# Two matmuls of 256 columns in place of one of 512 in a float32r kernel of an attention and two MLPs

## The chip, the cores and the metric

The kernel runs on one core of one Trainium2 chip. The metric is the device time of one execution in microseconds. A TensorE (PE) matmul multiplies a weight tile that lies in the array with the columns of a second tile; in the profile the loading of the weights has a row of its own, PEld. The other engines are VectorE (DVE), ScalarE (ACT), GpSimd (POOL) and SyncE (SP, which starts the DMAs here).

## What is computed

There are 12480 tokens with 128 channels. An attention with 32 inducing points goes over them twice, and two MLPs with 2048 hidden units follow:

```python
h = mab(I, x)                                   # 32 inducing points attend to all tokens
x = mab(x, h)                                   # the tokens attend to the 32 results
h = x @ w_in                                    # first MLP, 128 -> 2048
g = np.maximum(h, 0.0) + alpha * np.minimum(h, 0.0)
x = g @ w_out                                   # 2048 -> 128
h = np.maximum(x @ w2_in, 0.0)                  # second MLP, 128 -> 2048
return h * h @ w2_out                           # 2048 -> 128
```

`mab` is a softmax attention without projections.

## The kernel before

The tokens are cut into 25 tiles: 24 of T = 512 tokens and a last one of 192. A first stage, up to about 45 us, transposes the tokens (L244), computes the first attention and folds its result into the weights of the first MLP, so that this MLP can start from the attention weights `a_s` of a tile.

The main loop then runs in steps; step s handles one chunk of 128 hidden units of one tile, 16 chunks a tile and 400 steps' worth of chunks (25 x 16). All big products of the loop are in the type float32r, a fast form of float32 of lower precision. To keep the accuracy, an operand is split into two parts (`hi` and `lo`), and the function `three` (L588 to L591) forms a product from three matmuls into the same PSUM bank: weight hi x data hi, weight lo x data hi, weight hi x data lo. In each step, in this order:

- `l1_a` (matmul in L579) forms the chunk of the first hidden layer, one matmul, whose weights and data hold hi and lo parts in different partitions. ACT takes its relu into `g1h` (L583), DVE the remainder into `g1l` (L585).
- `l2_a`, 24 chunks behind, forms a chunk of the second hidden layer with `three`; ACT takes the relu `r` (L623), DVE multiplies to `sq` (L625).
- `l2_split` rounds `sq` to `g2h` on ACT (L632) and the remainder to `g2l` on POOL (L634).
- `l1_b`, 3 to 5 chunks behind `l1_a`, adds the chunk to the tile's first output (bank `y1`) with `three`.
- `l2_b`, 4 chunks behind `l2_a`, adds the chunk to the tile's second output (bank `y2`) with `three`; after the last chunk the tile is stored.

That is one matmul plus three times three, so ten matmuls of 512 columns in a step. Once a tile `end_y1` adds one more (L607), for the linear part of the first activation. A table (`plan`) puts the leftover work of the weights (conversion from the raw words, splitting, loads) and the attention of later tiles (L440 and following) between the steps, after their matmuls. The order of each engine is the order in which the code issues; nothing is rearranged. Every product writes a PSUM bank of its own of 512 float32 columns: two banks each for `h1`, `h2` and `y2`, one for `y1`. The profile leaves the numbers out of names, so `h` stands for both `h1` and `h2`, `y` for `y1` and `y2`.

Of the kernel before, what the change touches and what calls it, by code (L numbers as in the profile page):

```python
# [26 lines left out]
def attention_then_two_mlps(ctx: ExitStack, tc, x, inducing, w_in, w_out, alpha, w2_in, w2_out, out):  # L27
# [3 lines left out]
    nc = tc.nc  # L31
# [3 lines left out]
    P = 128  # L35
# [27 lines left out]
    def free_bank():  # L63
        turn[0] += 1
        return ms_bank() if turn[0] % 2 or main_loop else y2_bank()
# [3 lines left out]
    def keep_tile(name, shape, dt=F32):  # L69
        return keep.tile(shape, dt, name=name, tag=name)  # L70
# [35 lines left out]
    w1s = keep_tile("w1s", [P, DFF], F32R)  # L106
# [9 lines left out]
    v_s = keep_tile("v_s", [P, P], F32R)  # L116
# [132 lines left out]
    def scores(lhsT, tiles):  # L249
        b = free_bank()  # L250
        for i, t in enumerate(tiles):
            nc.tensor.matmul(  # L252
                b[i * M : (i + 1) * M, : geo[t][1]], lhsT, xt_cols(t), start=True, stop=True,
                tile_position=(0, i * M),
            )
        return b
# [82 lines left out]
    b = free_bank()  # L339
    nc.tensor.transpose(b[:, :M], ind, ident[:M, :M])  # L340
    nc.vector.tensor_copy(indT, b[:, :M])
    for g in range(last):
        b = scores(indT, groups[g])
# [31 lines left out]
    b = free_bank()  # L375
# [5 lines left out]
    b = scores(indT, groups[last])  # L381
# [4 lines left out]
    b = free_bank()  # L386
# [9 lines left out]
    b = free_bank()  # L396
# [11 lines left out]
    b = free_bank()  # L408
# [8 lines left out]
    b = y1_bank()  # L417
# [153 lines left out]
    y1_cur, y2_cur, y1_split = {}, {}, {}  # L571
    g1, g2, rr = {}, {}, {}

    def l1_a(i, other_bank):
        t, c = divmod(i, NCH)
        w = geo[t][1]
        b = h2_bank() if other_bank else h1_bank()
        a = a_s[t]
        nc.tensor.matmul(b[:, :w], w1s[: a.shape[0], c * P : (c + 1) * P], a[:, :w], start=True, stop=True)  # L579

        tag = "g2" if i < EARLY and i % 2 else "g1"
        hi = wk.tile([P, T], F32R, name="g1h", tag=tag + "h", bufs=4)[:, :w]
        nc.scalar.activation(hi, b[:, :w], AF.Relu)  # L583
        lo = wk.tile([P, T], F32R, name="g1l", tag=tag + "l", bufs=4)[:, :w]
        nc.vector.scalar_tensor_tensor(lo, b[:, :w], 0.0, f32(hi), op0=ALU.max, op1=ALU.subtract)  # L585
        g1[i] = hi, lo

    def three(b, w_hi, w_lo, hi, lo, start, stop):  # L588
        nc.tensor.matmul(b, w_hi, hi, start=start, stop=False)  # L589
        nc.tensor.matmul(b, w_lo, hi, start=False, stop=False)  # L590
        nc.tensor.matmul(b, w_hi, lo, start=False, stop=stop)  # L591

    def l1_b(i):
        t, c = divmod(i, NCH)
        if c == 0:
            y1_cur[t] = y1_bank() if t != 1 else y2_bank()
        b = y1_cur[t][:, : geo[t][1]]
        hi, lo = g1.pop(i)
        three(b, wo_hi[:, c, :], wo_lo[:, c, :], hi, lo, c == 0, False)
        if c == NCH - 1 and t:  # L600
            end_y1(t)

    def end_y1(t):
        w = geo[t][1]
        b = y1_cur.pop(t)[:, :w]
        a = a_s.pop(t)
        nc.tensor.matmul(b, v_s[: a.shape[0]], a[:, :w], start=False, stop=True)  # L607
        hi = wk.tile([P, T], F32R, name="y1h", tag="y1h", bufs=2)[:, :w]
        nc.scalar.copy(hi, b)
        lo = wk.tile([P, T], F32R, name="y1l", tag="y1l", bufs=2)[:, :w]  # L610
        nc.vector.tensor_tensor(lo, b, f32(hi), op=ALU.subtract)  # L611
        y1_split[t] = hi, lo

    def l2_a(i):
        t, c = divmod(i, NCH)
        w = geo[t][1]
        b = h2_bank()[:, :w]
        cols = slice(c * P, (c + 1) * P)
        three(b, w2[0][:, cols], w2[1][:, cols], *y1_split[t], True, True)
        if c == NCH - 1:  # L620
            del y1_split[t]
        r = wk.tile([P, T], F32, name="r", tag="r", bufs=2)[:, :w]
        nc.scalar.activation(r, b, AF.Relu)  # L623
        sq = wk.tile([P, T], F32, name="sq", tag="sq", bufs=3)[:, :w]
        nc.vector.tensor_tensor(sq, b, r, op=ALU.mult)  # L625
        rr[i] = sq
# [10 lines left out]
    def l2_b(i):  # L637
        t, c = divmod(i, NCH)
        t0, w, _, rs = geo[t]
        if c == 0:  # L640
            y2_cur[t] = y2_bank()
        b = y2_cur[t][:, :w]
        hi, lo = g2.pop(i)
        cols = slice(c * P, (c + 1) * P)
        three(b, w2[2][:, cols], w2[3][:, cols], hi, lo, c == 0, c == NCH - 1)
        if c == NCH - 1:


            o = wk.tile([P, T], F32, name="o", tag="o", bufs=2)[:, :w]
            nc.vector.transpose(o, b)  # L650
            del y2_cur[t]
            dst = out[t0 : t0 + w, :].rearrange("(b i r) (a j) -> a i r b j", i=M, j=M, r=rs)
            for a in range(P // M):
                nc.sync.dma_start(
                    out=dst[a], in_=o[a * M : (a + 1) * M, :].rearrange("i (r b j) -> i r b j", r=rs, j=M)
                )
# [36 lines left out]
    at(19, copy_u)  # L693
    at(20, step_v)
    at(22, end_y1, 0)
    for tiles in groups[1:]:
        for k, v in enumerate(second_attention(tiles)):
# [34 lines left out]
    for s in range(total + LAG2 + LAG2B + 4):  # L732
        if s < total:
            l1_a(s, s < LAG2 and s % 2)
        if 0 <= s - LAG2 < total:
            l2_a(s - LAG2)
        if 0 <= s - LAG2 - 1 < total:
            l2_split(s - LAG2 - 1)

        ends = [(l1_b, i) for i in l1_b_at.get(s, [])]  # L740
        if 0 <= s - LAG2 - LAG2B < total:
            ends.insert(0 if ends and ends[0][1] % NCH == 0 else len(ends), (l2_b, s - LAG2 - LAG2B))
        for f, i in ends:
            f(i)
        for f in plan.pop(s, []):
            f()
# [30 lines left out]
```

## Time and profile before

| what | us |
|---|---|
| median of 3 runs | 1006.49 (1006.4 to 1009.52) |
| the profiled execution, its time | 1006.87 |
| its span, first to last instruction | 1005.1 |
| PE busy in the span | 983.9 (98%) |
| DVE / ACT / POOL busy | 665.7 / 736.3 / 545.6 |

Matmuls are pipelined: the record of one ends after the next one's record has begun, so the listed durations add up to more than the time in which they ran. The distance from one start to the next is what a matmul takes from the engine. A weight load is listed apart and runs beside matmuls.

### The profile page before, as it was taken

Reading aid. Unit: us, or ns where it says so; the run is one execution under the profiler, and the core shown is the slowest. Engines: PE = TensorE matmul, PEld = TensorE weight load, DVE = VectorE, ACT = ScalarE, POOL = GpSimd, SP = SyncE. Lnnn points to the kernel's source line nnn. Section 1 sums busy time; section 2 is a strip of 40 time slices with the busy share of each in tenths; the row PEclk is TensorE's granted clock in tenths of the full one; section 3 lists DMA queues with packets and bytes.
Section 4 is the critical chain, followed back from the end, with each engine's and each line's share of the span. In section 5 each row is a group of like instructions: output and inputs, shape, how many; then the busy total and the mean of one; then the engine's idle time right before and its main releaser. Section 6 shows DMA issues by size and latency. Waiting matters only on the chain.

```text
span 1005.1 us, 13640 instructions
## 1 busy us (share of the span) xinstructions
PE 983.9 (98%) x4526; PEld 777.5 (77%) x4526; DVE 665.7 (66%) x1042; ACT 736.3 (73%) x1354; POOL 545.6 (54%) x436
## 2 busy tenths in 40 slices
PE   7879999999999999999999999999999999999997
PEld 5456788888788888788888788888788888788886
DVE  5799776666676666666666666666666666666556
ACT  5688877777777777777777777777777777777775
POOL 1346965555556555556555556555556555555560
PEclk9899999999999999999999999999999999999999
DMA  8513001100001100000100000100000200000000
GB/s 295 172 50 108 1 11 30 24 11 6 6 11 27 27 11 1 11 11 20 33 11 1 11 11 14 40 11 1 11 11 9 45 12 1 11 11 4 11 12 15
DMA packets 65062, 28.20 MB, mean 28 GB/s; under 512 B 53584, under 2 KB 57952, under 8 KB 64992
## 3 DMA queue, kind: packets, MB, share of 16 engines
q1 hardware_dynamic: 64992, 27.33, 10.9%
q8 instruction: 35, 0.57, 0.2%
q14 instruction: 35, 0.29, 0.1%
HBM read 14.80 MB, written 6.39 MB: 21 GB/s over the span
## 4 chain that ended last, share of the span: by engine, by line
PE 94%; DVE 3%; issue 1%; ACT 1%; DMA 0%; POOL 0%; SPq 0%; DVEq 0%; POOLq 0%; ACTq 0%
PE y L590 18%; PE y L591 18%; PE y L589 18%; PE h L589 9%; PE h L591 9%; PE h L590 9%; PE h L579 9%; PE h L244 1%; DVE g1l L585 1%; DVE mag L182 1%; PE ms L440 1%; PE y L607 1%; PE ms L252 0%; PE y L317 0%; DMA xg<-in_x_dram 0%
## 5 line engine op out<-in xcount | busy, mean ns | idle before, releaser
L634 POOL TENSOR_TENSOR g2l<-sq,g2h 128x512 fp32r<-128x512 f32 x376 | 487.7, 1297 | 370.1 <-ACT g2h L632 370.1
L585 DVE SCALAR_TENSOR_TENSOR g1l<-h,g1h 128x512 fp32r<-128x512 f32 (+1 forms) x400 | 269.5, 676 | 243.1 <-ACT g1h L583 239.9
L583 ACT ACTIVATE g1h<-h 128x512 fp32r<-128x512 f32 (+1 forms) x400 | 235.3, 589 | 164.4 <-PE h L579 162.7
L625 DVE TENSOR_TENSOR sq<-h,r 128x512 f32<-128x512 f32 (+1 forms) x400 | 270.8, 677 | 65.4 <-ACT r L623 8.9
L623 ACT ACTIVATE r<-h 128x512 f32<-128x512 f32 (+1 forms) x400 | 235.6, 589 | 72.3 <-PE h L591 71.6
L632 ACT CAST g2h<-sq 128x512 fp32r<-128x512 f32 (+1 forms) x400 | 240.5, 601 | 1.6 <-DVE sq L625 1.6
L579 PE MATMUL h<-a_s,w1s 128*128 128x512 f32 (+2 forms) x400 | 158.0, 396 | 6.3 <-DVE g1l L585 3.7
L589 PE MATMUL h<-y1h,w2i_hi 128*128 128x512 f32 (+1 forms) x400 | 157.7, 394 | 0.6 <-DVE g1l L585 0.3
L591 PE MATMUL h<-y1l,w2i_hi 128*128 128x512 f32 (+1 forms) x400 | 156.8, 392 | 0.4 <-DVE y1l L611 0.4
L589 PE MATMUL y<-g2h,w2o_hi 128*128 128x512 f32 (+1 forms) x400 | 157.0, 393 | 0.0
L591 PE MATMUL y<-g2l,w2o_hi 128*128 128x512 f32 (+1 forms) x400 | 156.9, 392 | 0.0
L590 PE MATMUL y<-g2h,w2o_lo 128*128 128x512 f32 (+1 forms) x400 | 156.8, 392 | 0.0
L590 PE MATMUL h<-y1h,w2i_lo 128*128 128x512 f32 (+1 forms) x400 | 156.7, 392 | 0.0
L590 PE MATMUL y<-g1h,wo_lo 128*128 128x512 f32 (+1 forms) x400 | 156.6, 392 | 0.0
L591 PE MATMUL y<-g1l,wo_hi 128*128 128x512 f32 (+1 forms) x400 | 156.6, 391 | 0.0
L589 PE MATMUL y<-g1h,wo_hi 128*128 128x512 f32 (+1 forms) x400 | 156.0, 390 | 0.0
L579 PEld LDWEIGHTS h<-a_s,w1s 128*128 128x128 f32 (+1 forms) x400 | 75.2, 188 | 32.2 <-DVE g1l L585 6.7
L589 PEld LDWEIGHTS h<-y1h,w2i_hi 128*128 128x128 f32 x400 | 75.4, 189 | 20.2 <-DVE sq L625 1.4
L590 PEld LDWEIGHTS y<-g1h,wo_lo 128*128 128x128 f32 x400 | 75.3, 188 | 18.5
L591 PEld LDWEIGHTS h<-y1l,w2i_hi 128*128 128x128 f32 x400 | 75.4, 188 | 18.4 <-DVE y1l L611 0.8
L589 PEld LDWEIGHTS y<-g1h,wo_hi 128*128 128x128 f32 x400 | 75.4, 188 | 18.3 <-ACT g1h L583 0.2
L591 PEld LDWEIGHTS y<-g2l,w2o_hi 128*128 128x128 f32 x400 | 75.4, 188 | 17.8
(128 smaller groups left out, 692.0 us busy)
## 6 DMA issues: line engine op xcount, KB each, us to landing
out_dram<-o SPq DMA_DIRECT2D x96, 64.0 KB, 2.2
xg<-in_x_dram SPq DMA_DIRECT2D x10, 512.0 KB, 7.0
raw<-in_moe_w_in_dram SPq DMA_DIRECT2D x8, 512.0 KB, 5.1
raw<-in_moe_w_out_dram SPq DMA_DIRECT2D x8, 512.0 KB, 3.9
a_s<-a_hi SPq DMA_DIRECT2D x46, 64.0 KB, 2.0
a_s<-a_lo SPq DMA_DIRECT2D x46, 64.0 KB, 2.0
xg<-in_x_dram SPq DMA_DIRECT2D x4, 256.0 KB, 3.8
xg<-in_x_dram SPq DMA_DIRECT2D x1, 96.0 KB, 4.0
```

Of the source, the lines that this page charges most:

```text
L182: nc.vector.scalar_tensor_tensor(c, v["h"], -(2**31), c, op0=ALU.bitwise_and, op1=ALU.bitwise_or)
L244: nc.tensor.transpose(b[:, r * p : (r + 1) * p], x_t[g][:p, i, r, :], ident[:p, :p])
L579: nc.tensor.matmul(b[:, :w], w1s[: a.shape[0], c * P : (c + 1) * P], a[:, :w], start=True, stop=True)
L583: nc.scalar.activation(hi, b[:, :w], AF.Relu)
L585: nc.vector.scalar_tensor_tensor(lo, b[:, :w], 0.0, f32(hi), op0=ALU.max, op1=ALU.subtract)
L589: nc.tensor.matmul(b, w_hi, hi, start=start, stop=False)
L590: nc.tensor.matmul(b, w_lo, hi, start=False, stop=False)
L591: nc.tensor.matmul(b, w_hi, lo, start=False, stop=stop)
L623: nc.scalar.activation(r, b, AF.Relu)
L625: nc.vector.tensor_tensor(sq, b, r, op=ALU.mult)
L632: nc.scalar.copy(hi, sq)
L634: (nc.vector if i >= total - LAG2 else nc.gpsimd).tensor_tensor(lo, sq, f32(hi), op=ALU.subtract)
```

## The change

A helper `passes` takes a bank and a list of products of a weight tile with a data tile. Where the bank is wider than 256 columns, it issues every product as two matmuls: the weights with the left half of the columns into the left half of the bank, then the same weights with the right half. All of them are one accumulation group: only the first matmul carries the start flag and only the last the stop flag. `three`, `l1_a` and `end_y1` go through it. The last tile, with 192 columns, is issued as before.

```diff
+    def passes(b, pairs, start, stop):
+        w = b.shape[1]
+        n = 2 if w > 256 else 1
+        todo = [
+            (b[:, k * w // n : (k + 1) * w // n], wt, a[:, k * w // n : (k + 1) * w // n])
+            for wt, a in pairs
+            for k in range(n)
+        ]
+        for k, (o, wt, a) in enumerate(todo):
+            nc.tensor.matmul(o, wt, a, start=start and k == 0, stop=stop and k == len(todo) - 1)
+
+    def three(b, w_hi, w_lo, hi, lo, start, stop):
+        passes(b, [(w_hi, hi), (w_lo, hi), (w_hi, lo)], start, stop)
...
-        nc.tensor.matmul(b[:, :w], w1s[: a.shape[0], c * P : (c + 1) * P], a[:, :w], start=True, stop=True)
+        passes(b[:, :w], [(w1s[: a.shape[0], c * P : (c + 1) * P], a[:, :w])], True, True)
...
-    def three(b, w_hi, w_lo, hi, lo, start, stop):
-        nc.tensor.matmul(b, w_hi, hi, start=start, stop=False)
-        nc.tensor.matmul(b, w_lo, hi, start=False, stop=False)
-        nc.tensor.matmul(b, w_hi, lo, start=False, stop=stop)
...
-        nc.tensor.matmul(b, v_s[: a.shape[0]], a[:, :w], start=False, stop=True)
+        passes(b, [(v_s[: a.shape[0]], a[:, :w])], False, True)
```

On PE, one step in the middle of the main loop reads so before (`y` with `g1h` is the tile's first output, `y` with `g2h` the second; each row is one matmul with its own weight load):

```order
L589 MATMUL y_5502<-g1h,wo_hi 128x512
L590 MATMUL y_5502<-g1h,wo_lo 128x512
L591 MATMUL y_5502<-g1l,wo_hi 128x512
L589 MATMUL y_5725<-g2h,w2o_hi 128x512
L590 MATMUL y_5725<-g2h,w2o_lo 128x512
L591 MATMUL y_5725<-g2l,w2o_hi 128x512
L579 MATMUL h_5825<-a_s,w1s 128x512
L589 MATMUL h_5831<-y1h,w2i_hi 128x512
L590 MATMUL h_5831<-y1h,w2i_lo 128x512
L591 MATMUL h_5831<-y1l,w2i_hi 128x512
```

and the same place after the change:

```order
L586 MATMUL y_7306<-g1h,wo_hi 128x256 x2
L586 MATMUL y_7306<-g1h,wo_lo 128x256 x2
L586 MATMUL y_7306<-g1l,wo_hi 128x256 x2
L586 MATMUL y_7619<-g2h,w2o_hi 128x256 x2
L586 MATMUL y_7619<-g2h,w2o_lo 128x256 x2
L586 MATMUL y_7619<-g2l,w2o_hi 128x256 x2
L586 MATMUL h_7762<-a_s,w1s 128x256 x2
L586 MATMUL h_7769<-y1h,w2i_hi 128x256 x2
L586 MATMUL h_7769<-y1h,w2i_lo 128x256 x2
L586 MATMUL h_7769<-y1l,w2i_hi 128x256 x2
```

Nothing changes place: each row becomes two matmuls behind each other with the same weights, all from one code line.

Near the end, where chunks of the last tile (192 columns) stand between those of the tile before, PE reads so before:

```order
L591 MATMUL y_10597<-g2l,w2o_hi 128x512
L589 MATMUL h_10807<-y1h,w2i_hi 128x192
L590 MATMUL h_10807<-y1h,w2i_lo 128x192
L591 MATMUL h_10807<-y1l,w2i_hi 128x192
L589 MATMUL y_10597<-g2h,w2o_hi 128x512
```

and after:

```order
L586 MATMUL y_14380<-g2l,w2o_hi 128x256 x2
L586 MATMUL h_14659<-y1h,w2i_hi 128x192
L586 MATMUL h_14659<-y1h,w2i_lo 128x192
L586 MATMUL h_14659<-y1l,w2i_hi 128x192
L586 MATMUL y_14380<-g2h,w2o_hi 128x256 x2
```

The narrow matmuls stay single. On ACT, DVE, POOL and SP the instructions, their order and their shapes are the same.

## Rows read from the trace of the kernel before

**Rows 1.** The page: span, busy time of PE, granted PE clock in 40 slices.

```profile
span 1005.1 us, 13640 instructions
...
PE 983.9 (98%) x4526; PEld 777.5 (77%) x4526; DVE 665.7 (66%) x1042; ACT 736.3 (73%) x1354; POOL 545.6 (54%) x436
...
PEclk9899999999999999999999999999999999999999
```

**Rows 2.** The page: the chain that ended last, shares of the span by engine.

```profile
PE 94%; DVE 3%; issue 1%; ACT 1%; DMA 0%; POOL 0%; SPq 0%; DVEq 0%; POOLq 0%; ACTq 0%
```

**Rows 3.** Windows: stretch, its length, busy time and count by engine, clock, DMA.

```profile
core 0: us, PE busy (x) PEld busy (x) DVE busy (x) ACT busy (x) POOL busy (x), PEclk, DMA share, GB/s
14.00:33.70 19.70, 19.70 (x245) 12.97 (x242) 14.32 (x33) 14.25 (x32) 3.92 (x3) 1.00 0.80 285
53.00:100.00 47.00, 40.66 (x174) 29.28 (x174) 45.96 (x69) 41.17 (x87) 27.44 (x22) 1.00 0.27 85
100.00:984.00 884.00, 883.90 (x3820) 706.80 (x3820) 571.58 (x851) 653.81 (x1167) 504.15 (x392) 1.00 0.07 14
989.40:998.80 9.40, 9.40 (x80) 9.07 (x78) 8.23 (x27) 7.06 (x25) 0.00 (x0) 1.00 0.18 28
```

**Rows 4.** Timeline, middle of the main loop: start us, duration us, engine, line.

```profile
500.33 0.40 PE L579 MATMUL h<-a_s,w1s 128*128 128x512 f32 x1
500.33 0.19 PEld L589 LDWEIGHTS h<-y1h,w2i_hi 128*128 128x128 f32 x1
...
500.57 0.39 PE L589 MATMUL h<-y1h,w2i_hi 128*128 128x512 f32 x1
500.57 0.19 PEld L590 LDWEIGHTS h<-y1h,w2i_lo 128*128 128x128 f32 x1
...
505.02 0.40 PE L579 MATMUL h<-a_s,w1s 128*128 128x512 f32 x1
```

**Rows 5.** Groups by line and shape, PE: count, busy us, mean ns, idle before.

```profile
L591 PE MATMUL y<-g1l,wo_hi 128*128 128x512 f32 x384 | 152.2, 396 | 0.0
L589 PE MATMUL y<-g1h,wo_hi 128*128 128x512 f32 x384 | 152.0, 396 | 0.0
L579 PE MATMUL h<-a_s,w1s 128*128 128x512 f32 x368 | 147.1, 400 | 0.2 <-DVE g1l L585 0.2
...
L607 PE MATMUL y<-a_s,v_s 128*128 128x512 f32 x23 | 9.1, 396 | 0.0
L579 PE MATMUL h<-a_s,w1s 96*128 96x512 f32 x16 | 6.8, 457 | 6.1 <-DVE g1l L585 3.5 <-DVE a_s L503 1.4 <-DVE w1s L518 1.2
...
L589 PE MATMUL y<-g1h,wo_hi 128*128 128x192 f32 x16 | 4.0, 252 | 0.0
...
L607 PE MATMUL y<-a_s,v_s 96*128 96x512 f32 x1 | 0.5, 502 | 0.4 <-DVE v_s L566 0.4
```

**Rows 6.** Timeline near the end, where 192 and 512 columns alternate; then 192 alone.

```profile
985.04 0.25 PE L589 MATMUL h<-y1h,w2i_hi 128*128 128x192 f32 x1
985.04 0.19 PEld L590 LDWEIGHTS h<-y1h,w2i_lo 128*128 128x128 f32 x1
985.13 0.27 PE L590 MATMUL h<-y1h,w2i_lo 128*128 128x192 f32 x1
985.15 0.19 PEld L591 LDWEIGHTS h<-y1l,w2i_hi 128*128 128x128 f32 x1
...
989.18 0.25 PE L589 MATMUL h<-y1h,w2i_hi 128*128 128x192 f32 x1
...
989.27 0.28 PE L590 MATMUL h<-y1h,w2i_lo 128*128 128x192 f32 x1
989.29 0.19 PEld L591 LDWEIGHTS h<-y1l,w2i_hi 128*128 128x128 f32 x1
...
989.96 0.19 PEld L591 LDWEIGHTS h<-y1l,w2i_hi 128*128 128x128 f32 x1
```

## Prediction

> **What bounds the kernel now.** I read the page first: the profiled execution spans 1005.1 us and PE is busy in 98% of it, with the granted clock at full speed (2.4 GHz, the upper of its two levels) in all slices but the second [rows 1]. Then the chain of work that ended last: 94% of the span lies on PE [rows 2]. Then the stretches. From 100 to 984 us PE is busy for 883.90 of 884.00 us, while DVE, ACT and POOL are busy for 572, 654 and 504 us of it [rows 3]. So in nine tenths of the span no other engine sets the pace: what a matmul takes from its start to the next one's start goes to the end of the kernel one for one. From 53 to 100 us, where the conversions of the weights share DVE and ACT with the loop, PE is busy for 40.66 of 47.00 us [rows 3]; there it sometimes waits, and part of what a matmul costs more disappears.
>
> The next reading is the true cost of a matmul. The mean of one is listed as 396 ns [rows 5], but neighbours overlap, so this is not what one costs. The start-to-start distance is. In the timeline, matmuls of l1_a two steps apart start at 500.33 and 505.02, with 20 matmuls of 512 columns between these starts: 4.69 us / 20 = 0.2345 us each [rows 4]. Every matmul has a weight load of its own, of 0.19 us by the records, which starts together with the matmul before it [rows 4]; it is covered as long as the matmul streams longer than the load takes.
>
> **The change part by part.** It takes away 3864 matmuls of 512 columns (nine products at 384 each, l1_a also 368 + 16, and end_y1 23 + 1 [rows 5]) and adds 7728 of 256 columns. The 161 of the last tile, 192 columns wide, stay as they are. Each new matmul brings its own weight load, so 3864 loads come in too, of weights that are already in the array. Nothing moves on ACT, DVE, POOL or SP; their order and tiles are the same. The term of the sum is therefore one number: twice the distance of two 256-column matmuls, less 0.2345 us.
>
> The trace has no 256-column matmul of this type, but it has the same products on both sides of that size: 512 columns, and 192 in the last tile. Near the end they alternate, and there two numbers can be told apart [rows 6].
>
> First, the stream. Where a 192-column matmul comes first after one of 512, its weights are already in. It starts at 985.04, and the load for the second one starts with it, as in the steady loop. The next matmul's record starts at 985.13, 0.09 us later; the last of five such places is 989.18 to 989.27, again 0.09. That is the time after which PE is through with a stream of 192 columns. Second, the load. That next matmul doesn't yet have its weights: the load for the third one, which in the steady loop starts with the second matmul, starts only at 985.15. In the stretch where all matmuls are 192 wide, loads start at 989.29 and, six loads on, at 989.96: 0.67 / 6 = 0.112 us each. So 192 columns are bound by the loads at 0.112 us, and not by the stream at 0.09.
>
> A straight line through the two streams, (192, 0.090) and (512, 0.2345), has a slope of 0.1445 / 320 = 0.452 ns a column and cuts off 3.3 ns. At 256 columns it gives 0.090 + 64 x 0.452 ns = 0.1189 us. The listed means say the same in another way: a 192-column matmul that waits for nothing is listed with 252 ns, one of 512 with 396, a slope of 144 / 320 = 0.450 ns a column [rows 5]. Both are above the 0.112 us of a load, so the stream stays the bound, by 7 ns, and the second load of the same weights is hidden under the matmul before it. If that cover were gone, each half would take the load's excess over 0.119 us.
>
> Thus a pair costs 2 x 0.1189 = 0.2378 us in place of 0.2345: 3.3 ns more. By the slope of the listed means, 256 x 0.450 ns down from 0.2345, a half would take 0.1193 us and a pair 4.1 ns more. Between 3.3 and 4.1 I take 3.5. It is in substance the fixed part of a matmul, the 3.3 ns of the line, paid a second time.
>
> The Trainium skill, "TensorE: Matmul & The Clock Gate", section "Back-to-back issue gap", gives N / 2.4 + 2.5 ns for a warm matmul. By it two halves cost 2.5 ns more than one whole; 3864 x 2.5 ns would be 9.7 us. The trace doesn't agree with its size for 512 columns (216 ns there, 234.5 here [rows 4]), but its form, a small fixed part, is that of the line.
>
> The sum: 136 of the 3864 pairs lie before 100 us and 3728 after. After: 3728 x 3.5 ns = 13.0 us. Before: at most 136 x 3.5 = 0.5 us, of which I keep 0.3, since PE waits there in part. Together 13.3 us. The profiled execution took 1006.87 us, 0.4 us over the median of the three runs shown (1006.49), and the cost lies inside its span; so it would become 1020.2 us, and the median 1019.8, which I call 1020.
>
> What else the change touches: the second half of a pair has no wait of its own that can stop it, since its operands are those of the first; the engine that reads a bank (ACT for g1h and r) gets it 3.5 ns later, which in a loop where ACT is busy for 654 of 884 us [rows 3] costs nothing. PE's sequencer must hand out twice as many instructions: one record per 0.1189 / 2 = 59 ns. From 14 to 33.7 us it handed out 245 matmuls and 242 loads in 19.7 us, 40 ns each [rows 3], over a stretch of some hundreds of instructions. So I take this at nothing.
>
> **Bounds.** Lowest, by rows: if the short stream were faster than the line and only loads bound it, 0.112 us a half, a pair would take 0.224 us, 10.5 ns less: 3864 x 10.5 = 41 us. Highest: if the 0.112 us of the 192-column matmul counted as its stream, the line through (192, 0.112) and (512, 0.2345) would give 0.1365 at 256, 38.5 ns more a pair: 149 us. I take a value near the lower middle, because the 0.09 us were read at five places where no load was in the way.
>
> **The rivals.** (1) Nothing happens: the time of a stream goes by columns alone, 0.458 ns each (0.2345 / 512), and two halves cost exactly one whole: 1006.5 us. For it: the fixed part is only 3.3 ns, of a size with the rounding of the rows. Against: 192 columns at 0.458 would be 0.088, and the rows say 0.09 every time. (2) Faster: what makes a 512-column matmul slow is something that a short stream doesn't meet, so that a half is bound by its load at 0.112 us alone: 1006.5 - 41 = 965 us. It decides as soon as a stream of 256 columns takes under 0.117 us. Against: at 192 columns the slope is already that of the long ones. (3) Much slower: the weight load isn't covered at 256 columns, because it can start only after the matmul before it has begun and its 7 ns of slack are eaten by jitter or a swap of weights; or the instruction supply sets the pace. Up to 0.1365 us a half by the bound above, 1155 us; with 5 ns lost per half, 1020 + 7728 x 5 ns = 1059 us. For it: loads would fill 0.112 of every 0.119 us. Against: in the 192-wide stretch loads follow each other at 0.112 us without falling behind, for 80 matmuls in 9.4 us [rows 3]. (4) The change doesn't do what it says: the second load of the same weights is skipped. Then rival 3 is impossible, and the time is my forecast's.
>
> The Trainium skill, in "TensorE: Matmul & The Clock Gate", section "Wait — 56ns, not 53.3ns?", states some 62 ns of the sequencer per matmul where the hardware decoder is off. If that held for loads as well, a half would take 124 ns and the total would be an estimated 1059 us; the 40 ns per record above speak against it.
>
> **How the numbers follow.** Forecast (1010 to 1035 us): 0.66. Rival 1, within 0.3% (1003.5 to 1009.5, about what a measurement of this kernel can tell from no change): 0.12. Rival 2: 0.04. Rival 3: 0.18, of which 0.08 below 1045 us. Rival 4 ends with the forecast. So faster 0.04, same 0.12, slower 0.84. The range from 1005 to 1045 us holds 0.66 + 0.11 + 0.08, and leaves out the gain and the large losses.
>
> **What would show it.** Right: in the timeline of the new kernel two matmuls of one pair start 0.119 us apart and pairs 0.238; PE stays busy in all of 100 to 984 us and the granted clock at full speed; loads start together with matmuls. Rival 1: pairs at 0.2345. Rival 2: pairs at 0.224, with loads starting after the matmuls' records, as in the 192-wide stretch now. Rival 3: the same lag of the loads, at pairs well over 0.238. Idle PE ahead of second halves would mean that waits or the instruction supply were overlooked, and would make the prediction wrong in its reason as well.

## The result, and the profile after

The changed kernel takes 1014.88 us (median of 4 runs, 1013.62 to 1016.28), the kernel before 1006.61: a ratio of 1.0068, 95% interval 1.0053 to 1.0083. It is slower, by 8.3 us, where 13.3 were forecast.

The page of the changed kernel (1014.82 us) has 3864 matmuls and as many weight loads more than [rows 1], and PE is as dominant in the chain as in [rows 2]:

```profile
span 1012.9 us, 21371 instructions
...
PE 991.6 (98%) x8390; PEld 964.5 (95%) x8390; DVE 666.2 (66%) x1042; ACT 737.3 (73%) x1354; POOL 545.1 (54%) x436
...
PEclk9899999999999999999999999999999999999999
...
PE 94%; DVE 3%; issue 1%; DMA 0%; ACT 0%; SPq 0%; POOL 0%; DVEq 0%; ACTq 0%; POOLq 0%
```

The windows (columns as in [rows 3]) show the same stretch of the main loop: PE is still busy in all but 0.2 of the 884 us, and the loads, whose listed 0.19 us overlap, now fill 878 of them.

```profile
100.00:984.00 884.00, 883.81 (x7487) 877.97 (x7488) 568.11 (x842) 651.28 (x1160) 505.62 (x394) 1.00 0.07 14
```

The timeline at the place of [rows 4], two halves to a row:

```profile
500.35 0.40 PE L586 MATMUL h<-a_s,w1s 128*128 128x256 f32 x2
500.47 0.30 PEld L586 LDWEIGHTS h<-y1h,w2i_hi 128*128 128x128 f32 x2
500.58 0.40 PE L586 MATMUL h<-y1h,w2i_hi 128*128 128x256 f32 x2
...
505.04 0.40 PE L586 MATMUL h<-a_s,w1s 128*128 128x256 f32 x2
```

Forty halves lie between the two starts of l1_a: 4.69 us / 40 = 0.1173 us, which is half of the 0.2345 us of a whole in [rows 4]. At this place the change costs nothing that two decimals show. The loss must come from elsewhere, and it has two main parts.

**A part in the loop that isn't the same in every tile.** The rows of ACT's g1h, one a step, measure the step. First tile 13, from its step 4 to its step 14, then tile 15, in the changed kernel:

```profile
538.57 0.60 ACT L600 ACTIVATE g1h<-h 128x512 fp32r<-128x512 f32 x1 [0.47 <-PE h L586]
...
562.03 0.60 ACT L600 ACTIVATE g1h<-h 128x512 fp32r<-128x512 f32 x1 [0.47 <-PE h L586]
...
615.40 0.60 ACT L600 ACTIVATE g1h<-h 128x512 fp32r<-128x512 f32 x1 [0.49 <-PE h L586]
...
639.14 0.60 ACT L600 ACTIVATE g1h<-h 128x512 fp32r<-128x512 f32 x1 [0.49 <-PE h L586]
```

Ten steps take 23.46 us in tile 13 and 23.74 us in tile 15; before rounding 2.347 and 2.373 us a step, 117.3 and 118.7 ns a half. In the kernel before the same ten steps take 23.43 us in both tiles:

```profile
533.80 0.60 ACT L583 ACTIVATE g1h<-h 128x512 fp32r<-128x512 f32 x1 [0.47 <-PE h L579]
...
557.23 0.60 ACT L583 ACTIVATE g1h<-h 128x512 fp32r<-128x512 f32 x1 [0.47 <-PE h L579]
...
610.43 0.60 ACT L583 ACTIVATE g1h<-h 128x512 fp32r<-128x512 f32 x1 [0.47 <-PE h L579]
...
633.86 0.60 ACT L583 ACTIVATE g1h<-h 128x512 fp32r<-128x512 f32 x1 [0.47 <-PE h L579]
```

From tile 2 to tile 23 there are just these two paces; a tile keeps one of them from its step 3 to its end, and the pace changes only behind end_y1 (step 2 of the next tile) or behind the scores of the attention (L440, step 0 of every fourth tile). Seven of these 22 tiles are slow. From step 3 to step 15 a slow tile takes 0.36 us more than in the kernel before, a fast one 0.04 us: together 3.2 us. Most of the remaining loss of the loop lies in the steps between these stretches, around end_y1 and the scores. From the first to the last g1h the loop takes 978.6 - 56.2 = 922.4 us against 971.1 - 53.7 = 917.4: 5.0 us more, 4.9 before rounding (rows in the next group).

**A part ahead of the loop.** The first g1h starts at 56.2 us in place of 53.7, though nothing ahead of it was changed. The first row is of the changed kernel, the second of the kernel before (a line's instructions: count, durations, first and last start):

```profile
L600 ACT ACTIVATE g1h<-h x400: 331/599/647, 56.2 to 978.6; 128x512 fp32r<-128x512 f32 x128, 128x192 fp32r<-128x192 f32 x6
```

```profile
L583 ACT ACTIVATE g1h<-h x400: 332/599/624, 53.7 to 971.1; 128x512 fp32r<-128x512 f32 x128, 128x192 fp32r<-128x192 f32 x6
```

The timeline shows where these 2.5 us arise. The second group of 16 transposes of the tokens takes 3.44 us in the changed kernel (first row) and 1.97 us in the kernel before (second):

```profile
11.53 3.44 PE L244 MATMUL h<-ident,xg 128*128 128x128 f32 x16
```

```profile
10.39 1.97 PE L244 MATMUL h<-ident,xg 128*128 128x128 f32 x16
```

The rest of the difference of the spans, 7.8 - 5.0 - 2.5 = 0.3 us by these rounded numbers and 0.45 us in the trace, lies behind the last g1h.

### The profile page after: what moved, and what is told of

It is laid out like the page before. It is cut to its first block, busy times and chain, and to the rows that moved or that the text cites. A ratio compares the mean times of both kernels' runs of the same rounds, so it can differ in the third digit from the quotient of the medians.

```text
span 1012.9 us, 21371 instructions
## 1 busy us (share of the span) xinstructions
PE 991.6 (98%) x8390; PEld 964.5 (95%) x8390; DVE 666.2 (66%) x1042; ACT 737.3 (73%) x1354; POOL 545.1 (54%) x436
## 4 chain that ended last, share of the span: by engine, by line
PE 94%; DVE 3%; issue 1%; DMA 0%; ACT 0%; SPq 0%; POOL 0%; DVEq 0%; ACTq 0%; POOLq 0%
PE y L586 54%; PE h L586 36%; PE h L244 1%; DVE g1l L602 1%; DVE mag L182 1%; PE ms L440 1%; DMA xg<-in_x_dram 0%; PE y L252 0%; PE ms L252 0%; PE y L317 0%; PE y L553 0%; PE h L513 0%; PE y L306 0%; DVE sq L637 0%; DVE w1s L518 0%
## 5 line engine op out<-in xcount | busy, mean ns | idle before, releaser
L586 PE MATMUL h<-a_s,w1s 128*128 128x256 f32 (+2 forms) x784 | 159.2, 283 | 6.2 <-DVE g1l L602 3.6
L586 PE MATMUL h<-y1h,w2i_hi 128*128 128x256 f32 (+1 forms) x784 | 158.4, 281 | 0.8 <-DVE g1l L602 0.3
L586 PE MATMUL h<-y1l,w2i_hi 128*128 128x256 f32 (+1 forms) x784 | 157.5, 280 | 0.4 <-DVE y1l L623 0.4
L586 PE MATMUL y<-g2h,w2o_hi 128*128 128x256 f32 (+1 forms) x784 | 157.6, 281 | 0.0
L586 PE MATMUL y<-g1h,wo_lo 128*128 128x256 f32 (+1 forms) x784 | 157.6, 280 | 0.0
L586 PE MATMUL y<-g2h,w2o_lo 128*128 128x256 f32 (+1 forms) x784 | 157.4, 280 | 0.0
L586 PE MATMUL h<-y1h,w2i_lo 128*128 128x256 f32 (+1 forms) x784 | 157.2, 280 | 0.0
L586 PE MATMUL y<-g1l,wo_hi 128*128 128x256 f32 (+1 forms) x784 | 157.1, 280 | 0.0
L586 PE MATMUL y<-g2l,w2o_hi 128*128 128x256 f32 (+1 forms) x784 | 156.9, 280 | 0.0
L586 PE MATMUL y<-g1h,wo_hi 128*128 128x256 f32 (+1 forms) x784 | 156.4, 279 | 0.0
```

Of the source, the lines that this page charges most:

```text
L586: nc.tensor.matmul(o, wt, a, start=start and k == 0, stop=stop and k == len(todo) - 1)
```

## Experiments

The question was what a half really costs (a fixed part for each matmul, its columns, or the load beside it), what makes the second pace, and whether the late start belongs to the change.

### The changed kernel twice more, and the kernel before once more

No edit. The first of these runs:

> The changed kernel once more, unaltered. Theory of the pace: in the first profile, steps of the main loop took either 2.347 or 2.373 us (117.3 or 118.7 ns a half) and kept the one or the other for a whole tile, from the step after end_y1 to the next end_y1; before, every step took 2.343 on the mean. If this is a property of the program, the same two paces come back, the loop from its first l1_a to its last is about 5 us longer than before, and the whole is 1.005 to 1.008 times the kernel before. Rival (fixed part per matmul): one single pace, some 1.4 ns a pair over 234.3. Theory of the start: the first g1h began at 56.15 us instead of 53.66; if the doubled program causes this, it is at 56 again; if it is chance, it varies between runs and the ratio comes out nearer to 1.005.

1015.68 us (1012.76 to 1016.84), ratio 1.0079 (1.0064 to 1.0093). Both paces came back with the same lengths, and so did the late start: first g1h at 56.4 us, the loop 979.6 - 56.4 = 923.2 us long.

> The kernel before once more, unaltered. If the start of the first profile (first g1h at 53.66 us) is a property of that program, it comes back within some tenths of a us; if the start varies by chance, it moves by one or two us. Steps of the main loop at 2.343 us on the mean in every tile, 234.3 ns a matmul, by all theories.

1006.51 us (one run); the first g1h at 53.3 us, the loop 970.8 - 53.3 = 917.5 us as before, and ten steps take 23.43 us in every tile from 2 to 23.

> The changed kernel a third time, for its start and for the pace of its tiles. If the late rise of the clock is chance, it comes in part of the executions of both kernels, and the runs of each fall into two groups about 2.3 us apart; the loop from its first to its last g1h is 5 to 6 us longer than before in any case. If the doubled number of matmuls causes the late rise, the changed kernel's first g1h is at 56 us again.

1014.18 us (1012.48 to 1015.68), ratio 1.0064 (1.0050 to 1.0077). Its rows for tiles 13 and 15, as above:

```profile
536.70 0.60 ACT L600 ACTIVATE g1h<-h 128x512 fp32r<-128x512 f32 x1 [0.50 <-PE h L586]
...
560.43 0.60 ACT L600 ACTIVATE g1h<-h 128x512 fp32r<-128x512 f32 x1 [0.49 <-PE h L586]
...
614.27 0.60 ACT L600 ACTIVATE g1h<-h 128x512 fp32r<-128x512 f32 x1 [0.47 <-PE h L586]
...
637.74 0.60 ACT L600 ACTIVATE g1h<-h 128x512 fp32r<-128x512 f32 x1 [0.48 <-PE h L586]
```

Now tile 13 is the slow one (23.73 us) and tile 15 the fast one (23.47 us), the other way round than in the first profile, in the same program. So the program, with a tile's buffers and the work planned beside it, doesn't fix the tile's pace. It is handed on: in all three profiles from tile 3 on the order of fast and slow tiles repeats every eight tiles, and in the two later ones (nine slow tiles) it is shifted by four tiles against the first. What remains is how the matmuls fall in time; on what they fall is not shown. The start is an early one this time, in the same program, with the loop 977.1 - 53.8 = 923.3 us long:

```profile
L600 ACT ACTIVATE g1h<-h x400: 330/599/641, 53.8 to 977.1; 128x512 fp32r<-128x512 f32 x128, 128x192 fp32r<-128x192 f32 x6
```

and its second group of transposes, in the timeline, is as quick as that of the kernel before:

```profile
10.42 1.97 PE L244 MATMUL h<-ident,xg 128*128 128x128 f32 x16
```

So the late start isn't a property of the changed program. The trace shows what it is. Its record of the granted clock begins, at full speed (2.4 GHz), at 8.9 us in the first profile of the kernel before, at 14.6 us in that of the changed kernel and at 9.1 us in this one. Ahead of it the page and the windows fill in full speed, so the first digit of PEclk in [rows 1] is in part no reading. The transposes show the clock there: up to where the record begins they start 0.213 us apart, behind it 0.109 us, about the ratio of the two levels (1.2 and 2.4 GHz). By 9.1 us PE had done the same work in all three, the first 16 transposes, from some 3.5 us on. In the first profile of the changed kernel nearly all of the second group lies ahead of the record. In the profile of the kernel before with l1_a's product in halves (below) the record begins at 13.0 us, within the group, and from there on the same transposes are the quick ones:

```profile
11.99 2.45 PE L244 MATMUL h<-ident,xg 128*128 128x128 f32 x16
```

Of all 14 profiles kept, the record begins at 8.5 to 9.1 us in six, with the first g1h at 53.3 to 53.8 us, and at 13.0 to 14.9 us in eight, with the first g1h at 54.0 to 56.4 us. The eight include variants of the kernel before; the kernel before itself was profiled twice, both times with an early start. The 11 runs of it that were timed beside the first repetition fall into 1006.1 to 1006.9 and 1007.7 to 1008.7 us, and the 16 of the changed kernel into 1012.5 to 1013.7 and 1014.7 to 1016.8, but the two later sets of the kernel before (17 and 23 runs, 1006.1 to 1010.2) show no such groups. That the kernel before sometimes starts late as well fits its spread, but neither of its two profiles shows it. What decides between the two starts stays open.

### Halves in another order

```diff
         todo = [
             (b[:, k * w // n : (k + 1) * w // n], wt, a[:, k * w // n : (k + 1) * w // n])
-            for wt, a in pairs
             for k in range(n)
+            for wt, a in pairs
         ]
```

> All products of a group on the left half first, then all on the right half, so that neighbouring matmuls have different weights and write the same half. Theory that a matmul's time goes by its columns, with a small extra that depends on how the matmuls fall in time: 117.3 or 118.7 ns a half again, total within 3 us of the changed kernel. Rival (loading the weights that are already there is cheaper, or switching halves costs): the steps become longer or shorter by more than 1 ns a half, over 7 us in all.

1014.23 us (1013.12 to 1016.33), ratio 1.0070 (1.0057 to 1.0083): as the changed kernel. Steps take 2.347 or 2.373 us again, the loop 977.0 - 53.6 = 923.4 us. Whether neighbours share their weights or their half of the bank makes no difference.

### Other cuts

All three replace the two equal halves by a cut at a fixed column, 264 here:

```diff
-        n = 2 if w > 256 else 1
-        todo = [
-            (b[:, k * w // n : (k + 1) * w // n], wt, a[:, k * w // n : (k + 1) * w // n])
-            for wt, a in pairs
-            for k in range(n)
-        ]
+        cuts = [0, 264, w] if w > 256 else [0, w]
+        todo = [
+            (b[:, lo:hi], wt, a[:, lo:hi])
+            for wt, a in pairs
+            for lo, hi in zip(cuts, cuts[1:])
+        ]
```

> The pair cut at 264 instead of 256: 264 and 248 columns. By columns alone, 264 x 0.4583 = 121.0 and 248 x 0.4583 = 113.7 ns, 234.7 a pair, steps of 2.347 us, total about 1009 to 1011 if the slower pace of 2.373 doesn't appear with these widths, and as the changed kernel if it does. If a fixed part per matmul is the cause, the total is that of the changed kernel, 1014 to 1015. If the load of the weights needs more than 113.7 ns from start to start, the 248 columns are held up and the total exceeds that of the changed kernel.

1021.92 us (1020.47 to 1022.46), ratio 1.0142 (1.0129 to 1.0155). Steps take 2.378 us on the mean of ten in every tile, 237.8 ns a pair; the expected 2.347 doesn't appear anywhere.

> The pair cut at 272: 272 and 240 columns, between the last two. By columns alone 234.7 ns. With a floor of 111.5 ns, 124.7 + 111.5 = 236.2, total about 1013 to 1015. If what 264 and 248 columns cost (237.8 ns a pair, 2.378 us a step) was a load that holds up the narrow half at about 116.8 ns, the pair takes 124.7 + 116.8 = 241.5, steps of 2.415 us, total about 1034.

1021.65 us (one run), again 2.378 us a step: neither 236.2 nor 241.5 ns a pair but 237.8. The timeline shows the single pieces, since the load for the next product starts with the narrow piece (PEld rows):

```profile
500.03 0.40 PE L583 MATMUL y<-g2h,w2o_hi 128*128 128x272 f32 x2
500.16 0.30 PEld L583 LDWEIGHTS y<-g2h,w2o_lo 128*128 128x128 f32 x2
500.27 0.40 PE L583 MATMUL y<-g2h,w2o_lo 128*128 128x272 f32 x2
500.40 0.30 PEld L583 LDWEIGHTS y<-g2l,w2o_hi 128*128 128x128 f32 x2
```

The narrow piece takes 0.11 us (0.16 to 0.27), what its 240 columns give at 0.4583 ns each; the wide one takes 0.13, 3 to 5 ns more than its 272 columns give. So a load that holds up the narrow piece at 116.8 ns is ruled out; why two unequal pieces cost 3 ns more than two equal ones at the fast pace stays open (that a piece starts at a column other than 256 is a cause that was not tested apart).

> The pair cut at 320: 320 and 192 columns. By columns alone, 234.7 ns a pair and a total near the changed kernel's. If the weight load sets a floor from start to start, the 192 columns take the floor: at the 111.5 ns read in the 192-wide stretch of the kernel before, 146.7 + 111.5 = 258.2 ns a pair, steps of 2.58 us, total 1006.7 + 3864 x 0.0239 = 1099 us.

1091.05 us (one run); ten pairs take 2.567 us. Starts of the 320-column pieces in the timeline (the row's second matmul is the 192-column piece):

```profile
500.19 0.42 PE L583 MATMUL y<-g1h,wo_hi 128*128 128x320 f32 x2
500.44 0.42 PE L583 MATMUL y<-g1h,wo_lo 128*128 128x320 f32 x2
500.70 0.42 PE L583 MATMUL y<-g1l,wo_hi 128*128 128x320 f32 x2
500.95 0.42 PE L583 MATMUL y<-g2h,w2o_hi 128*128 128x320 f32 x2
```

0.76 / 3 = 0.253 by these rows, 0.2567 over ten steps, against 0.2347 by columns and an expected 0.2582. The load does set a floor: 256.7 - 320 x 0.4583 = 110 ns for the 192-column piece, near the 112 ns of [rows 6]. In the trace's nanoseconds the loads themselves start by turns 108 to 109 and 146 to 150 ns apart, while the 192-column piece's own record is followed by the next one after 85 to 88 ns, which is its columns: it is the next weights that are late. This is the wall beside which the change runs: below some 240 columns (an estimate, 110 / 0.4583) a piece costs a load and no longer its columns.

### Halves among wholes

```diff
-        nc.tensor.matmul(b, w_lo, hi, start=False, stop=False)
+        nc.tensor.matmul(b[:, : min(256, b.shape[1])], w_lo, hi[:, : min(256, b.shape[1])], start=False, stop=False)
```

> The kernel before with the second of the three products (weights' low part) on the left 256 columns alone: 1152 of 3864 matmuls are halves, single ones among whole ones, and their other half is left out of the computation. It measures one half where no other half stands beside it. By columns alone 117.1 to 117.3 ns from its start to the next: total about 1006.7 - 1152 x 0.117 = 872 us. With a fixed part of 3.3 ns, as predicted, 118.9 ns and about 874 us; the distance from start to start in the timeline decides.

The kernel leaves out the right half of that product. 873.59 us (one run); steps of 1.980 us (468.67 to 488.47 for ten):

```profile
468.67 0.60 ACT L583 ACTIVATE g1h<-h 128x512 fp32r<-128x512 f32 x1 [0.23 <-PE h L579]
...
488.47 0.60 ACT L583 ACTIVATE g1h<-h 128x512 fp32r<-128x512 f32 x1 [0.23 <-PE h L579]
```

The total lies between the two that were expected, 872 and 874 us, nearer to that of the fixed part, but runs of one kernel differ by more than that. The distance from start to start, which was to decide, doesn't either: in the trace it is 116 to 121 ns for a half, but the whole behind it then takes some 230 in place of 234. The sum of a step is free of this: seven wholes at 234.3 ns leave 1980 - 1640 = 340 ns for three halves, 113.3 each, less than half of a whole and less than a half of the changed kernel at either pace. So one price for each width doesn't give both kernels' times; it matters how halves and wholes stand among each other.

Then the same product in two halves, all work done:

```diff
-        nc.tensor.matmul(b, w_lo, hi, start=False, stop=False)
+        w = b.shape[1]
+        n = 2 if w > 256 else 1
+        for k in range(n):
+            cols = slice(k * w // n, (k + 1) * w // n)
+            nc.tensor.matmul(b[:, cols], w_lo, hi[:, cols], start=False, stop=False)
```

> The kernel before with only the second of the three products of `three` in halves: 1152 pairs among 2712 wholes, all work done. If a matmul costs what its own width costs (234.3 ns a whole, 117.3 to 118.7 a half), 13 matmuls of a step take 2.344 to 2.352 us and the total is 1007 to 1010 us. If the time depends on how the matmuls fall behind one another, as the kernel with single halves suggests (steps of 1.980 us, 0.455 ns a column where wholes alone take 0.4576), a step can take 0.455 x 5120 = 2.330 us, and the total would be about 1001 to 1002 us, faster than both kernels. The predicted fixed part of 3.3 ns a pair would give 2.353 us a step and 1010 to 1011 us.

1009.97 us (1008.64 to 1011.95), ratio 1.0021 (1.0012 to 1.0030). All tiles run at 2.347 us a step, as here in tile 13:

```profile
536.09 0.60 ACT L583 ACTIVATE g1h<-h 128x512 fp32r<-128x512 f32 x1 [0.47 <-PE h L579]
...
559.56 0.60 ACT L583 ACTIVATE g1h<-h 128x512 fp32r<-128x512 f32 x1 [0.47 <-PE h L579]
```

The hoped-for gain of the mixture didn't come, and the predicted fixed part (2.353) didn't either. Three pairs a step cost as much as ten do at the fast pace: 2.347 against 2.343 us. So what a step loses at the fast pace, 3.6 ns, isn't a price per additional matmul.

Last, l1_a's product alone in halves:

```diff
-        nc.tensor.matmul(b[:, :w], w1s[: a.shape[0], c * P : (c + 1) * P], a[:, :w], start=True, stop=True)
+        n = 2 if w > 256 else 1
+        for k in range(n):
+            nc.tensor.matmul(
+                b[:, k * w // n : (k + 1) * w // n], w1s[: a.shape[0], c * P : (c + 1) * P],
+                a[:, k * w // n : (k + 1) * w // n], start=k == 0, stop=k == n - 1,
+            )
```

> The kernel before with only l1_a's product in halves: 384 pairs, 11 matmuls a step. By own widths, steps of 2.343 to 2.347 us and a total of 1006.5 to 1008.5 us; with the predicted fixed part of 3.3 ns a pair, 1008; if the time depends on the mixture, up to 0.6% less, steps down to 2.330 us and about 1001 us at the lowest.

1008.88 us (1007.17 to 1011.84), ratio 1.0012 (1.0001 to 1.0022). Tiles run at 2.343 or at 2.347 us a step, by turns. No mixture beats the kernel before.

### One more half in a tile

```diff
         a = a_s[t]
+        if c == 8 and 0 < t < NT - 1:
+            nc.tensor.matmul(b[:, :256], w1s[:, c * P : (c + 1) * P], a[:, :256], start=True, stop=True)
         passes(b[:, :w], [(w1s[: a.shape[0], c * P : (c + 1) * P], a[:, :w])], True, True)
```

> The changed kernel with one more matmul of 256 columns in each of 23 tiles (the left half of l1_a's chunk 8 is formed twice, with the same result). Cost by any theory 23 x 0.118 = 2.7 us. What it tells: whether the pace of a tile (2.347 or 2.373 us a step) belongs to the tile (its buffers, its neighbours in other engines) or to how the matmuls fall in time. If to the timing, the pace changes at the step of the additional matmul in a part of the tiles, in the middle of the tile, as it does now behind end_y1, which adds two halves. If to the tile, it stays from step 3 to the end of the tile as in the changed kernel.

1017.34 us (one run). The step with the additional half is 0.118 us longer in fast tiles and 0.120 in slow ones, as expected, but the pace stayed the same behind it in all tiles; it changed only behind end_y1 and the scores, as before. By its expectation this outcome speaks for the tile; against it stand the repeated runs, in which one and the same tile of one program has either pace. The additional half didn't leave the paces alone: from tile 5 on their order now repeats every four tiles, two fast and two slow, in place of every eight. A reason why the pace doesn't change at once, for example that one more half in an unbroken train of equal halves shifts the train against nothing, was not tested.

### Earlier work for PE at the start

```diff
+    z = st_tile("z", [P, P])
+    nc.vector.memset(z, 0.0)
+    warm = ms_bank()
+    for _ in range(6):
+        nc.tensor.matmul(warm[:, :P], z, z, start=True, stop=True)
     ident = st_tile("ident", [P, P])
```

> The kernel before with six small matmuls of zeros at its very start, while the first tokens are on their way; their result is not used. In the profiles so far the granted clock rises to full speed either about 8.6 to 8.9 us or 13 to 15 us after the start, and the second case loses some 2.5 us until the main loop. If the rise depends on how early PE becomes busy, it comes by about 5 to 6 us with the added work, in all executions: the first g1h at 51.5 to 53 us, the median 1004.5 to 1006 and the spread of the runs below 1 us. If the rise doesn't depend on it, the total is that of the kernel before.

1007.75 us (1005.62 to 1010.42), ratio 1.0000 (0.9989 to 1.0012). The runs spread as widely as without the addition, where less than 1 us was expected, and the profiled execution has a late start: the record of the clock begins at 13.8 us, and the first g1h is at 54.2 us. Six matmuls of zeros from 1 to 4 us don't bring the faster start; data other than zeros weren't tried.

## Why the prediction was right, and where it wasn't

**The bound** was read rightly: PE was idle for 0.1 of 884 us in the loop before ([rows 3]) and is for 0.2 after, so what the halves take more appears in the time.

**The cover of the loads** held as predicted. Loads fill 878 of 884 us and follow each other without falling behind, and the cut at 320 columns showed the floor where the 192-wide stretch [rows 6] had put it: 110 ns measured, 112 read. Nearly all loads start 2 to 4 ns behind a matmul, in fast and in slow tiles alike, so the rivals of a lost cover and of the instruction supply fall as the forecast had them; whether either has a part in the slow pace is not shown. The Trainium skill, "TensorE: Matmul & The Clock Gate", section "LDWEIGHTS (loading the stationary operand)", gives columns / 1.2, an estimated 107 ns for 128 columns; the floor of 110 ns agrees within 4 ns.

**The size of the term** was too large, and its reason was wrong. The step that failed is the straight line through the streams of 192 and 512 columns: it cut off 3.3 ns as a fixed part of each matmul, and the prediction took 3.5 ns a pair from it. Between numbers of 0.09 and 0.2345 us, the first with two decimals, such a remainder isn't to be had: 0.088 instead of 0.090 would have made it nil. In the trace's nanoseconds the 21 places of the kernel before, where 192 columns come behind 512, scatter from 86 to 92, and the 192-column pieces of the cut at 320 take 85 to 88. The second support, the slope of the listed means, doesn't hold either: halves are listed with some 281 ns, where that line puts them (252 + 64 x 0.450 = 281), and yet start 117.3 ns apart. A listed duration says little of what a matmul takes from the engine.

What the runs showed in place of a fixed part is two paces. At the fast pace a pair takes 234.7 ns, 0.4 more than a whole, and a step is as long with 3 pairs as with 10. At the slow pace a pair takes 237.3, 3.0 ns more than a whole. By the prediction's own signs a slow tile reads as the forecast (0.237 us a pair against 0.238) and a fast tile as rival 1 (0.2347 against 0.2345); since the same program gives the same tile either of the two, neither is the price of a matmul. In the loop this gave 4.9 us in the first profile (5.7 to 5.9 in the later ones) in place of the forecast 13.3: 1.3 ns a pair over the 3797 between the first and the last g1h.

**Rival 1**, columns alone, was nearer in its mechanism than the forecast: at the fast pace 5120 columns in 2.3467 us are 0.4583 ns each, the rival's 0.458. Its time missed because of the slow pace, which no row of the kernel before shows, and which the runs place in trains of equal halves.

**What filled the rest** of the 8.3 us was not in the prediction: about 2.5 us of the profiled difference are a start that came late. It is not the change's doing, as the third profile of the changed kernel shows. Early start against early start, that profile's span of 1011.4 us stands against 1005.1 and 1004.7 of the kernel before: the change itself costs 6.3 to 6.7 us, 0.6 to 0.7%, of which 0.4 us lie behind the last g1h. The medians of the result carry a part of the start beside it.

So the forecast named the bound and the cover rightly, and its direction came true for a reason that the runs refute, a fixed part of each matmul. That the measured 8.3 us are not further from 13.3 is luck: the change itself cost half of it, and a late start was added. Open are what the two paces lock to, and what decides the start.

## What to carry to other kernels

Where PE is the bound and the next weights load under the running matmul, cutting a float32r matmul in two equal halves costs little as long as each half streams longer than a load (110 ns here): 0.6 to 0.7% in this kernel. Unequal pieces can cost more with each piece still as long as a load, 1.4% at 264 and 248 columns, and where a piece streams shorter than a load it costs a load, some 84 us more in this kernel at 320 and 192 columns. A remainder of a few ns from a line through two rounded numbers isn't a price: find a third width, or bound it by zero on one side. Look at the start of the main loop in both profiles before crediting a change with the whole difference.

## What the runs showed of the hardware that wasn't expected

- At the full granted clock (2.4 GHz), trains of equal float32r halves take 0.4583 ns a column, 1.10 cycles, or 0.4635, and keep one of the two for some 16 steps, in an order of tiles that repeats; wholes take 0.4576.
- Two unequal pieces (264 and 248, 272 and 240 columns) cost 237.8 ns a pair in all tiles, more than two equal halves at the fast pace (234.7), though both pieces are longer than, or as long as, a load.
- With the same program the granted clock's record begins at full speed at 9.1 us in one execution and at 14.6 or 14.9 us in others; the transposes ahead of it start 0.213 us apart, those behind it 0.109 us, and the first g1h moves from 53.8 to 56.2 or 56.4 us.
